# Reordering the two ends of a fused top-k attention and squared-ReLU kernel: one chunk of q turned ahead of k, and another order of the last step's work

## The chip, the cores and the metric

The kernel runs on one core of one Trainium2 chip. The metric is the device time of one execution in microseconds (us). Its engines are TensorE (PE, matrix multiply, with weight loads shown apart as PEld), VectorE (DVE), ScalarE (ACT), GpSimd (POOL) and SyncE (SP, which here only issues DMA). Each engine works through its own queue in order; semaphores tie the queues together.

## The reference

Top-k attention over 8 batches of 8 heads with 576 positions of 64 elements, followed by a feed-forward layer with a squared ReLU:

```python
B, H, S, D = q.shape                     # 8, 8, 576, 64
top_k = 32
scores = scale * np.matmul(q, k.transpose(0, 1, 3, 2))
kth = np.partition(scores, -top_k, axis=-1)[..., -top_k:-top_k + 1]
scores = np.where(scores >= kth, scores, -1000000000.0)
scores = scores - np.max(scores, axis=-1, keepdims=True)
attn = np.exp(scores)
attn = attn / (np.sum(attn, axis=-1, keepdims=True) + 1e-09)
x = np.matmul(attn, v)                   # then laid out as 4608 tokens x 512
h = np.maximum(x @ w_in, 0.0)            # w_in 512 x 2048
out = h * h @ w_out                      # w_out 2048 x 512
```

## The kernel before, in words

The work is cut into 144 steps (`U`). A step takes two tiles of 128 query rows (mostly the two heads of a pair, for one chunk `c` of the rows) against all 576 keys. For step u these things happen, each a function of its own:

- `prep_units(i)` turns the q and k of head pair i by PE transposes (L134 for the 128-row chunks, L146 for the last 64 rows) and copies them with a scale into `qkT` (L136 on DVE for the very first k, L138 and L149 on ACT for all others).
- `scores(u)` multiplies q with k in float32 into the two PSUM banks `sc_b` and `sc_a` (L202), and ACT copies them to SBUF as `s` (L207).
- `split(u)`, `join(u)` and `mins(u)` sort the 576 scores of a row into larger and smaller halves (DVE L238 to L250, POOL L257 to L269); `bring(u)` lets PE put a part of them back into PSUM (L223).
- `topk(u)` finds the 32 largest in four rounds of MAX8 (L288) and MATCH_REPLACE8 (L292) on DVE; the last round's MAX8 reads all 576 columns.
- `below(u, x)` marks what is under the threshold (ACT L334), `expo(u, x)` takes the exponentials of half x (ACT L343), `mask(u)` joins both (POOL L339), `turn(u)` transposes the weights by DMA into `wT`.
- `products(u)` multiplies them with v (PE L410: ten matmuls of 65 columns), `invert` takes the reciprocal of the sums (DVE L415, L421), `place` writes the scaled result into `x_tok` (ACT L438).

The feed-forward layer runs beside this in pieces: an "up" piece is 8 or 16 matmuls with `w_in` (PE L512) into one of two `gen` buffers, whose evacuation (`bend`: ACT L518, ReLU into `rl`) and square (POOL L526 or ACT L523) are put on the list `late` and written out by `flush()`. A "down" piece is four matmuls with `w_out` (PE L540) into the bank `dn_ps`; the last of four is followed by its own evacuation (ACT L547), also by way of `late`. Where there is no piece, `idle_piece()` lets PE multiply constants into `dn_ps` (L559).

There is no planner at run time. The program text is the order of every queue, and `pin` keeps it. There are three parts. Ahead of the loops, pair 0 is turned and the first two steps' scores are made. The first loop covers u below `Z` = 125, the second one u from 125 to 141. The last two steps, 142 and 143, are written out by hand. In step 143 the weights do not go through POOL and DMA: DVE masks them (`mask_last`, L377), PE transposes them (`turn_last`, L392), and ACT and DVE copy one half each (L395, L397). The last 128 tokens' feed-forward part is spread over the k-dimension as well: `x_last((kh,))` transposes one quarter of the tokens' 512 elements (PE L884, ACT L886), and `ups_last(bank, kh)` adds that quarter's eight matmuls (PE L891) into the two score banks, which are called `one` and `two` there. When all four quarters are in, `square_last` (ACT L896, DVE L898) and 32 final matmuls (PE L966) follow. `verify`, `note` (DVE L304, POOL L313 to L315) and the reductions at L947 to L950 gather flags that say whether the fast path's assumptions held.

The beginning ahead of the loops, in the order of the text:

```python
soon, coming = prep_units(0), 1
for _ in range(4):
    soon.pop(0)()
scores(0)
split(0)
join(0)
mins(0)
catch_up()
scores(1)
```

Of the kernel before, what the change touches and what calls it, by code (L numbers as in the profile page):

```python
# [22 lines left out]
def kernel(  # L23
# [22 lines left out]
    def pin(ins):  # L46
        tc.keep_in_program_order(ins)
        return ins
# [74 lines left out]
    def prep_units(i):  # L123
        q_raw, k_raw, v_raw = raw[i]
        qkT = heads.tile([128, 2, S], f32, name="qkT")
        va = vau[i % 6]
        prep[i] = (qkT, va)

        def main(which, src):
            def go():  # L130
                very_first = i == 0 and which == 1
                tp = ps_one.tile([128, 512], f32, name="gen", bufs=2)
                for c in range(4):
                    pin(nc.tensor.transpose(tp[:, c * 128:(c + 1) * 128], src[:, c], id_f[:, :]))  # L134
                if very_first:
                    pin(nc.vector.tensor_scalar(qkT[:, which, 0:512], tp[:, :], scalar1=EACH, scalar2=None, op0=ALU.mult))  # L136
                else:
                    pin(nc.scalar.activation(qkT[:, which, 0:512], tp[:, :], AF.Copy, scale=EACH))  # L138
                    owe(A=0.5)
            return go  # L140

        def rest(both=(0, 1), bank=None):
            tp = ps_one.tile([128, 512], f32, name="gen", bufs=2) if bank is None else bank
            for which in both:
                src = (q_raw, k_raw)[which]
                pin(nc.tensor.transpose(tp[:, which * 64:(which + 1) * 64], src[0:64, 4], id_f[0:64, 0:64]))  # L146
            owe(A=0.25)
            at = slice(both[0], both[-1] + 1)
            pin(nc.scalar.activation(qkT[:, at, 512:576], tp[:, 64 * both[0]:64 * both[-1] + 64].rearrange("p (w n) -> p w n", n=64), AF.Copy, scale=EACH))  # L149

        def values():
            owe(G=0.76)
            assert i < 6 or av_left[i - 6] == 0
            pin(nc.gpsimd.tensor_copy(va[:, :, :, 0:64], v_raw[:, :]))

        if i == 0:
            return [main(0, q_raw), main(1, k_raw), lambda: rest((1,), sc[0][:, 0, :]), values, lambda: rest((0,))]
        return [main(0, q_raw), main(1, k_raw), rest, values]


# [202 lines left out]
    def flush():  # L363
        while late:
            late.pop(0)()
# [281 lines left out]
    OLD = 2 * (U - GROUP)  # L647
    w_loads, w_casts = weight_units()
    scores(0)
    split(0)  # L650
    join(0)
    mins(0)
# [24 lines left out]
    for u in range(Z):  # L677
        now[0] = u
        f = u - 4
        lead = 2 if u > DEEP + 2 else 1  # L680
        pass_step()
        owe(A=4.5 if u < DEEP + 15 else 4.12, G=2.92)
        if u > 0:
            below(u - 1, 0)
        if u == 0:
            topk(0, (0, 1))
            split(1)
            join(1)
            topk(0, (2, 3))
        elif not DEEP < u < DEEP + 3:  # L690
            split(u + lead)
        if not DEEP < u < DEEP + 3:
            ahead(u + 1 + lead)
        if u > 0:
            topk(u, (0,))
        if u == DEEP + 2:
            join(u + 1)
            split(u + 2)
            ahead(u + 3)
            bring(u + 2)  # L700
        if ok(f) and f % 2:
            invert_two(f)
        if ok(f - 1):
            place(f - 1)
        if checks:
            note()
        if u == DEEP + 2:
            mins(u + 2)
        elif u != DEEP + 1:
            mins(u + lead)  # L710
        if u < DEEP + 3:
            catch_up()
# [36 lines left out]
        if u == DEEP:  # L749
            mins(u + 2)  # L750
            catch_up()
            ahead(u + 3)
            bring(u + 2)
        for _ in range(2 if u < 8 or u in (U - 22, U - 19) else 1):
            prepare(u)
        if 1 < u < 24 and not ups and not downs:
            idle_piece(2)
        turn_x(u)
        if w_casts and u >= 4:
            w_casts.pop(0)()  # L760
        if w_loads and u >= 1:
            w_loads.pop(0)()
# [9 lines left out]
    for u in range(Z, U - 2):  # L772
# [39 lines left out]
        expo(u, 0)  # L812
        if u == U - 4:
            piece()
            flush()
        expo(u, 1)
        flush()
        if u == Z:
# [52 lines left out]
        at = w[:, x, 0:S].bitcast(i32)  # L871
        pin(nc.gpsimd.tensor_tensor(at, at, marks[u % 2][:, x, :].bitcast(i32), op=ALU.add))
    turn(u)
    bend()
    square()
    empty(two)

    xl = ffp.tile([128, KH, 128], bf16, name="xT_1", bufs=2)
# [9 lines left out]
    def up_last(hp, f0, khs):  # L888
        for kh in khs:
            for n in range(4):  # L890
                pin(nc.tensor.matmul(out=hp[:, n * 128:(n + 1) * 128], lhsT=w_in[:, kh, (f0 + n) * 128:(f0 + n + 1) * 128],  # L891
                                     rhs=xl[:, kh, :], start=False, stop=(kh == 2 and n == 3)))

    def square_last(z, bank):
        rl = ffp.tile([128, 512], f32, name="rl", bufs=4)
# [20 lines left out]
    topk(u, (0, 1))  # L916
    expo_last(0)
    expo_last(1)
    bend()
    square()  # L920
    ups_last(one, 0)
    ups_last(two, 0)
    downs.pop(0)()
    topk(u, (2, 3))
    invert(u - 2)
    place(u - 2)
    mask_last(0)
    mask_last(1)
    turn_last(0)
    turn_last(1)  # L930
    x_last((1,))
    st[u]["o"] = ps_one.tile([128, 512], f32, name="gen", bufs=2)[:, 0:130].rearrange("p (x d) -> p x d", x=2)
    products(u)
    products(u - 1)
    invert(u)
    place_last(u)
    invert(u - 1)
    place_last(u - 1)
    x_last((3,))
    ups_last(one, 1)  # L940
    x_last((2,))
    ups_last(two, 1)
    ups_last(one, 3)
    ups_last(two, 3)
    verify(u)
    note()
    pin(nc.vector.tensor_reduce(worst[:, 0:1], flags[:, :, 0:OLD], axis=mybir.AxisListType.XY, op=ALU.max))  # L947
    sums_checked(nc.vector, OLD, 2 * U)
    pin(nc.vector.tensor_reduce(worst[:, 1:2], flags[:, :, OLD:2 * U], axis=mybir.AxisListType.XY, op=ALU.max))
    pin(nc.vector.tensor_scalar(worst[:, 0:1], worst[:, 0:1], scalar1=worst[:, 1:2], scalar2=0.0, op0=ALU.max, op1=ALU.is_gt))  # L950
    for z, bank in ((0, one), (2, two)):
        ups_last(bank, 2)
        for j in range(2):
            square_last(z + j, bank[:, j, :])
    downs.pop(0)()
# [144 lines left out]
```

## Time and profile before

| What | us |
|---|---|
| Median of 3 runs | 868.44 (867.41 to 871.32) |
| The profiled execution itself | 870.59 |
| Its span, from the first to the last instruction | 868.8 |
| DVE busy in the span | 837.7 (96%) |
| ACT busy | 810.6 (93%) |
| POOL busy | 797.5 (92%) |
| PE busy | 761.5 (88%) |

A line of a timeline gives start, duration, engine, source line, operation, written tile and read tiles with their shapes, the number of instructions merged, and in brackets the idle time in front of it with what ended it. A line of a table by stretches gives for each engine the busy time and, in brackets, the instructions; then the TensorE clock that was granted (1.00 is full), the share of the DMA engines and what they moved. Where a line of one source line's statistics appears, it gives the shortest, the median and the longest duration in ns, and the first and the last start. Matmul ends are modelled, so successive starts are the better measure of PE's pace.

### The profile page before, as it was taken

What the parts mean: (1) busy time and instruction counts of PE and PEld (TensorE: products, weight loads), DVE (VectorE), ACT (ScalarE), POOL (GpSimd) and SP (SyncE); (2) the same over time, 40 slices, a digit from 0 to 9 for tenths busy, and PEclk for the clock granted to TensorE, in tenths of its full rate; (3) what the DMA queues carried; (4) which work ended last, traced back from release to release, by engine and by line L of the source; (5) the groups of instructions that cost most, each with busy time, mean ns of one, the idle gap of its engine ahead of it and who ended that gap; (6) DMA issues with size and microseconds to landing.
All of it is one profiled execution on the core that took longest, in us unless ns stands there. A gap on an engine that the chain in (4) does not pass through costs nothing.

```text
span 868.8 us, 20017 instructions
## 1 busy us (share of the span) xinstructions
PE 761.5 (88%) x6038; PEld 484.6 (56%) x6038; DVE 837.7 (96%) x3427; ACT 810.6 (93%) x1635; POOL 797.5 (92%) x748
## 2 busy tenths in 40 slices
PE   6998997888888988889889888889898998999986
PEld 3554555555555545556555555556555654666654
DVE  5999999999999999999999999999999999999994
ACT  2887999999999999999999999999999999999982
POOL 3788999999999999999999999999999998999761
PEclk8999999999999999999999999999999999999998
DMA  5597776546556666356554565654565545423341
GB/s 122 125 228 156 185 172 109 121 101 114 95 106 114 120 120 121 67 112 121 109 120 96 113 115 98 124 116 105 114 128 109 117 100 107 87 58 86 73 84 44
DMA packets 325444, 98.06 MB, mean 113 GB/s; under 512 B 317520, under 2 KB 317776, under 8 KB 325328
## 3 DMA queue, kind: packets, MB, share of 16 engines
q1 hardware_dynamic: 323984, 96.28, 54.5%
q8 instruction: 49, 0.80, 0.4%
q14 instruction: 67, 0.55, 0.2%
q10 hardware_dynamic: 1344, 0.43, 0.2%
HBM read 36.70 MB, written 9.44 MB: 53 GB/s over the span
## 4 chain that ended last, share of the span: by engine, by line
DVE 56%; issue 12%; POOL 12%; PE 12%; ACT 7%; DMA 1%; SPq 0%; DVEq 0%; ACTq 0%; POOLq 0%
DVE m L288 25%; DVE cat L292 15%; DVE tops L238 7%; DVE cat L250 6%; POOL cat L257 5%; POOL cat L265 3%; ACT s L207 2%; PE sc_b L223 2%; PE sc_b L202 2%; PE gen L512 1%; POOL cat L269 1%; PE av_ps L410 1%; PE dn_ps L559 1%; ACT h L523 1%; PE dn_ps L540 1%
## 5 line engine op out<-in xcount | busy, mean ns | idle before, releaser
L288 DVE MAX8 m<-cat 128x8 f32<-128x100 f32 (+3 forms) x1152 | 435.1, 419 | 0.1
L292 DVE MATCH_REPLACE8 cat<-m,cat 128x100 f32<-128x100 f32 (+2 forms) x864 | 259.3, 308 | 0.3 <-issue 0.3
L265 POOL TENSOR_TENSOR cat<-s 128x576 int32<-128x576 int32 (+1 forms) x144 | 196.1, 1362 | 7.4 <-ACT s L207 7.1
L257 POOL TENSOR_TENSOR cat<-cat,tops 128x576 int32<-128x576 int32 (+1 forms) x144 | 196.0, 1361 | 1.9 <-DVE tops L238 0.8
L202 PE MATMUL sc_b<-qkT 64*128 64x288 f32 (+1 forms) x640 | 119.0, 449 | 33.7 <-DVE cat L250 24.3
L540 PE MATMUL dn_ps<-w_out,h 128*128 128x512 bf16 x560 | 143.3, 381 | 1.9 <-ACT wide L547 1.9
L223 PE MATMUL sc_b<-tops,id_f 128*128 128x144 f32 x528 | 96.6, 306 | 50.5 <-ACT s L207 50.2
L512 PE MATMUL gen<-xT,w_in 128*128 128x256 bf16 (+1 forms) x1088 | 128.5, 264 | 1.9 <-ACT rl L518 1.2
L512 PEld LDWEIGHTS <-w_in 128*128 128x128 bf16 x1344 | 109.9, 98 | 32.8 <-issue 19.9
L223 PEld LDWEIGHTS sc_b<-tops,id_f 128*128 128x128 f32 x528 | 73.4, 189 | 93.8 <-ACT s L207 90.3
L410 PEld LDWEIGHTS <-wT 128*128 128x128 bf16 (+3 forms) x1600 | 98.1, 99 | 47.0 <-issue 8.5
L334 ACT ACTIVATE marks_a<-s,m 128x576 bf16<-128x576 f32 x144 | 115.8, 812 | 0.0
L334 ACT ACTIVATE marks_b<-s,m 128x576 bf16<-128x576 f32 x142 | 110.4, 783 | 0.0
L202 PE MATMUL sc_a<-qkT 64*128 64x288 f32 (+1 forms) x640 | 109.1, 420 | 0.9 <-DVE tops L238 0.9
L207 ACT ACTIVATE s<-sc_b 128x576 f32<-128x576 f32 x144 | 94.8, 659 | 14.0 <-PE sc_b L202 8.6
L207 ACT ACTIVATE s<-sc_a 128x576 f32<-128x576 f32 x144 | 95.9, 666 | 6.6 <-PE sc_a L202 3.8
L238 DVE TENSOR_TENSOR tops<-sc_a,s 128x576 f32<-128x576 f32 x132 | 98.5, 746 | 0.0
L540 PEld LDWEIGHTS <-h 128*128 128x128 bf16 x560 | 47.7, 98 | 68.6 <-issue 31.3
L250 DVE TENSOR_TENSOR cat<-sc_b,tops 128x288 f32<-128x288 f32 x191 | 80.8, 443 | 5.2 <-PE sc_b L223 4.7
L518 ACT ACTIVATE rl<-gen 128x512 f32<-128x512 f32 x140 | 83.9, 599 | 1.0 <-PE gen L512 0.9
L202 PEld LDWEIGHTS sc_b<-qkT 64*128 64x128 f32 (+1 forms) x640 | 48.3, 176 | 61.6 <-DVE cat L250 33.2
L269 POOL TENSOR_TENSOR cat<-tops 128x288 int32<-128x288 int32 x97 | 77.8, 802 | 0.0
(133 smaller groups left out, 1358.4 us busy)
## 6 DMA issues: line engine op xcount, KB each, us to landing
out_dram<-wide SPq DMA_DIRECT2D x31, 256.0 KB, 2.7
q_raw<-in_q_dram SPq DMA_DIRECT2D x30, 256.0 KB, 3.7
k_raw<-in_k_dram SPq DMA_DIRECT2D x30, 256.0 KB, 3.7
h<-in_moe_w_in_dram SPq DMA_DIRECT2D x8, 512.0 KB, 5.3
h<-in_moe_w_out_dram SPq DMA_DIRECT2D x8, 512.0 KB, 4.2
v_raw_a<-in_v_dram SPq DMA_DIRECT2D x15, 256.0 KB, 4.1
v_raw_b<-in_v_dram SPq DMA_DIRECT2D x15, 256.0 KB, 4.0
out_dram<-wide SPq DMA_DIRECT2D x9, 128.0 KB, 2.5
```

The lines of the kernel that those rows point to most:

```text
L202: pin(nc.tensor.matmul(out=sc[j][r if rest else slice(0, 128), x, 0:HALF], lhsT=qkT[r, 0, c * 128:min(S, (c + 1) * 128)], rhs=qkT[r, 1, j ...
L207: pin(nc.scalar.activation(s[:, :, j * HALF:(j + 1) * HALF], sc[j][:, :, 0:HALF], AF.Copy))
L223: pin(nc.tensor.matmul(out=far[:, x, :], lhsT=id_f[:, :], rhs=st[w]["tops"][:, x, QUAR:HALF], start=True, stop=True))
L238: pin(tt(tops[:, :, :], one, two, op=ALU.max))
L250: pin(nc.vector.tensor_tensor(d["cat"][:, :, lo:lo + QUAR], far, d["tops"][:, :, 0:QUAR], op=op))
L257: pin(nc.gpsimd.tensor_tensor(at, at, top, op=ALU.subtract))
L265: pin(nc.gpsimd.tensor_tensor(at, s[:, :, 0:n], s[:, :, HALF:HALF + n], op=ALU.add))
L288: pin(nc.vector.max(out=m[r][:, x, :], in_=cat[:, x, at]))
L292: pin(nc.vector.match_replace(out=cat[:, x, at], in_to_replace=m[r][:, x, :], in_values=cat[:, x, at], imm_value=NEG))
L334: pin(nc.scalar.activation(marks[u % 2][:, x, :], d["s"][:, x, :], AF.Relu, bias=d["m"][3][:, x, 7:8], scale=-1.0))
L512: pin(nc.tensor.matmul(out=hp[:, n * n_rows:(n + 1) * n_rows], lhsT=w_in[:, kh, (f0 + n) * 128:(f0 + n + 1) * 128], rhs=xt(kh), start=(kh ...
L540: pin(nc.tensor.matmul(out=op[:, :], lhsT=held["h2"][:, f, c * 128:(c + 1) * 128], rhs=w_out[:, f, :], start=(f == 0), stop=(f == NF - 1)))
```

## The change

Four places change.

1. At the beginning only chunk 0 of q is transposed ahead of k, and copied by ACT as 128 columns. Chunks 1 to 3 are transposed behind the first scores (`soon.pop(0)()` behind `scores(0)`) and copied as 384 columns, between ACT's two score copies of step 0.
2. In step 0 an `idle_piece()`, four matmuls of 512 columns, goes in front of the scores of step 2.
3. In the second loop `flush()` is called between `expo(u, 0)` and `expo(u, 1)` in every step, where it was called in step 140 alone.
4. In the last two steps the order is changed: both pending `bend` and `square` calls come in step 142; the reciprocal of step 141 goes ahead of DVE's last round; `x_last((1,))` goes ahead of `turn_last(0)`, and `ups_last(one, 1)` between the two `turn_last`; `verify` and `note` go behind the masks; the products, reciprocals and placings of step 142 come ahead of those of 143; the quarters follow as 2, 3 with the matmuls of quarter 3 last.

```diff
-        def main(which, src):
+        def main(which, src, c0=0, c1=4):
...
-                for c in range(4):
+                at = slice(c0 * 128, c1 * 128)
+                for c in range(c0, c1):
...
-            return [main(0, q_raw), main(1, k_raw), lambda: rest((1,), sc[0][:, 0, :]), values, lambda: rest((0,))]
+            return [main(0, q_raw, 0, 1), main(1, k_raw), lambda: rest((1,), sc[0][:, 0, :]), values, main(0, q_raw, 1, 4), lambda: rest((0,))]
...
     scores(0)
+    soon.pop(0)()
     split(0)
...
             split(u + lead)
+        if u == 0:
+            idle_piece()
         if not DEEP < u < DEEP + 3:
             ahead(u + 1 + lead)
...
         expo(u, 0)
         if u == U - 4:
             piece()
-            flush()
+        flush()
         expo(u, 1)
...
     turn(u)
-    bend()
-    square()
+    for _ in range(2):
+        bend()
+        square()
     empty(two)
...
     expo_last(0)
     expo_last(1)
-    bend()
-    square()
     ups_last(one, 0)
     ups_last(two, 0)
     downs.pop(0)()
-    topk(u, (2, 3))
-    invert(u - 2)
+    topk(u, (2,), lambda: invert(u - 2))
+    topk(u, (3,))
     place(u - 2)
+    x_last((1,))
     mask_last(0)
     mask_last(1)
+    verify(u)
+    note()
     turn_last(0)
+    ups_last(one, 1)
     turn_last(1)
-    x_last((1,))
+    products(u - 1)
     st[u]["o"] = ...
     products(u)
-    products(u - 1)
+    invert(u - 1)
+    place_last(u - 1)
     invert(u)
     place_last(u)
-    invert(u - 1)
-    place_last(u - 1)
-    x_last((3,))
-    ups_last(one, 1)
     x_last((2,))
     ups_last(two, 1)
-    ups_last(one, 3)
-    ups_last(two, 3)
-    verify(u)
-    note()
+    x_last((3,))
+    ups_last(one, 2)
+    ups_last(two, 2)
...
     for z, bank in ((0, one), (2, two)):
-        ups_last(bank, 2)
+        ups_last(bank, 3)
```

More of the change, by code (lines that the diff above doesn't have):

```diff
@@ L132, in go @@
                 tp = ps_one.tile([128, 512], f32, name="gen", bufs=2)
-                for c in range(4):
+                at = slice(c0 * 128, c1 * 128)
+                for c in range(c0, c1):
                     pin(nc.tensor.transpose(tp[:, c * 128:(c + 1) * 128], src[:, c], id_f[:, :]))
                 if very_first:
-                    pin(nc.vector.tensor_scalar(qkT[:, which, 0:512], tp[:, :], scalar1=EACH, scalar2=None, op0=ALU.mult))
+                    pin(nc.vector.tensor_scalar(qkT[:, which, at], tp[:, at], scalar1=EACH, scalar2=None, op0=ALU.mult))
                 else:
-                    pin(nc.scalar.activation(qkT[:, which, 0:512], tp[:, :], AF.Copy, scale=EACH))
+                    pin(nc.scalar.activation(qkT[:, which, at], tp[:, at], AF.Copy, scale=EACH))
                     owe(A=0.5)
@@ L891, in up_last @@
                 pin(nc.tensor.matmul(out=hp[:, n * 128:(n + 1) * 128], lhsT=w_in[:, kh, (f0 + n) * 128:(f0 + n + 1) * 128],
-                                     rhs=xl[:, kh, :], start=False, stop=(kh == 2 and n == 3)))
+                                     rhs=xl[:, kh, :], start=False, stop=(kh == KH - 1 and n == 3)))
     def square_last(z, bank):
```

## The prediction

> **What bounds the kernel now.** I read the page first, then the busy time by stretches, then the chain that ended last, then the timelines of the first 35 us and the last 25 us, where the diff works. The profiled execution took 870.59 us, its span 868.8 us, so 1.8 us lie around it; it stands 2.15 us above the median of the three runs, 868.44 us.
>
> ```profile
> core 0: us, PE busy (x) PEld busy (x) DVE busy (x) ACT busy (x) POOL busy (x), PEclk, DMA share, GB/s
> 100.00:735.00 635.00, 555.30 (x4410) 355.44 (x4410) 631.93 (x2599) 626.48 (x1268) 625.35 (x574) 1.00 0.57 114
> 735.00:810.00 75.00, 71.54 (x619) 48.55 (x620) 70.04 (x293) 71.90 (x151) 72.75 (x67) 0.98 0.35 73
> 850.00:869.00 19.00, 11.27 (x114) 9.18 (x114) 6.60 (x16) 4.02 (x11) 0.78 (x3) 0.86 0.10 32
> ```
>
> From 100 to 735 us DVE is busy 631.93 of 635 us, with ACT and POOL close behind; to 810 us POOL, ACT and PE are each over 95%. These long stretches are a belt: what reaches them earlier leaves them earlier, and nothing in the diff shortens them. Only ahead of the belt and behind it (850 to 869 us, DVE busy 6.60 of 19) is there time that order alone can change. The built order agrees: POOL and SP keep their order to the last instruction, DVE differs in a few places behind step 142, PE and ACT at the head, ACT in nine steps of the second loop, PE in the tail.
>
> **Head: k 0.33 us earlier.** In the chain, q's landing releases eight transposes (L134), then DVE's copy of k, then the first scores.
>
> ```profile
> L134 PE MATMUL gen<-id_f,q_raw x4: 351/418/444, 6.0 to 6.7; 128*128 128x128 f32 x4
> L134 PE MATMUL gen<-id_f,k_raw x4: 272/273/273, 6.9 to 7.2; 128*128 128x128 f32 x4
> 7.54 0.69 DVE L136 TENSOR_SCALAR qkT<-gen 128x512 f32<-128x512 f32 x1 [7.54 <-PE gen L134]
> 8.37 0.76 PE L202 MATMUL sc_b<-qkT 64*128 64x288 f32 x4 [0.67 <-DVE qkT L136]
> 8.93 0.68 PE L202 MATMUL sc_a<-qkT 64*128 64x288 f32 x4
> 11.91 0.76 PE L202 MATMUL sc_b<-qkT 64*128 64x288 f32 x4 [2.29 <-ACT s L207]
> ```
>
> The four of q start 0.22 us apart (6.04 to 6.71), the four of k 0.11 (6.90 to 7.23): PE speeds up near 6.9 us. With three q transposes gone, k's start at 6.28, 6.5, 6.7 and 6.9, the last 0.33 us before 7.23; DVE's copy, the scores and everything behind follow. (If the speed-up came first, 3 x 0.11 = 0.33 too; if after, 3 x 0.22 = 0.66.) The three transposes moved behind the first scores, and their copy on ACT, lie between the end of the scores at 9.61 and the second scores at 11.91, 2.29 us in which PE only waits: 0.33 us on PE, and on ACT less than the 0.69 that DVE takes for 512 columns, say 0.6, ahead of a copy that waits for DVE's third split operation anyway. Cost: nothing; without that cover 0.33 + 0.6, some 0.9 us. No DMA moves.
>
> **Head: the idle piece.** Four 128x512 matmuls go in behind the second scores, ahead of the q tail and the third scores.
>
> ```profile
> 13.00:14.00 1.00, 0.17 (x3) 0.00 (x0) 1.00 (x5) 0.35 (x1) 0.53 (x1) 0.84 0.00 0
> 14.00:15.00 1.00, 0.00 (x0) 0.00 (x0) 1.00 (x4) 0.34 (x1) 0.00 (x0) 0.50 0.14 33
> 15.45 1.33 PE L202 MATMUL sc_b<-qkT 64*128 64x288 f32 x4 [2.28 <-ACT qkT L149]
> 16.54 1.20 PE L202 MATMUL sc_a<-qkT 64*128 64x288 f32 x4
> 17.67 3.40 PE L559 MATMUL dn_ps<-fill,id_h 128*128 128x512 bf16 x8
> 18.46 0.47 DVE L240 TENSOR_TENSOR sc_b<-sc_a,s 128x288 f32<-128x288 f32 x1 [0.39 <-ACT s L207]
> 30.59 0.82 DVE L250 TENSOR_TENSOR cat<-sc_b,tops 128x288 f32<-128x288 f32 x2 [0.62 <-PE sc_b L223]
> ```
>
> PE stands 2.28 us, and the granted clock falls to 0.50 at 13.7 us (a mean of 0.84 over its microsecond). Under it the third scores start 1.09 us apart instead of the 0.56 of the first ones (8.37 to 8.93), DVE waits 0.39 us for their copy, and the eight fillers take 3.40 us (0.43 each), which sends the next pair's copies, and with them ACT's whole queue, late; the 0.62 us before 30.59 is that lateness arriving at DVE. The new matmuls take 4 x 0.43 = 1.7 us at worst, within the 2.28. If they hold the clock, both waits go: 0.39 + 0.62 = 1.01 us. Bounds 0 and 1.01; I take 1.01: from 11.91 to 15.45 PE works some 1.3 of 3.5 us now, and with the fillers 2.2 (at full clock) to 3.0. The Trainium skill, "TensorE: Matmul & The Clock Gate", section "What's actually happening", lets the clock fall only after a window of some 3.4 us of idling; by it these 2.28 us cost nothing, the fillers bring nothing and the sum below would be 2.8 us. The trace disagrees: 0.50 within 2.28 us of waiting.
>
> **Second loop: bend between the two exps.** `flush()` now runs in every step between `expo(u, 0)` and `expo(u, 1)`; nine times an L518 or L547 evacuation moves ahead of the second exp, four times an L523 square with it. ACT's sum per step is the same; no wait is added if the PE piece is done by then.
>
> ```profile
> 776.35 1.04 PE L540 MATMUL dn_ps<-w_out,h 128*128 128x512 bf16 x4
> 777.88 0.76 PE L223 MATMUL sc_b<-tops,id_f 128*128 128x144 f32 x4 [0.50 <-ACT s L207]
> 778.72 0.89 ACT L343 ACTIVATE w_two_a<-s,low 128x576 bf16<-128x576 f32 x1
> 780.23 0.17 DVE L415 RECIPROCAL shares<-av_ps 128x2 f32<-128x2 f32 x1 [0.94 <-PE av_ps L410]
> DVE cat L250 <- PE sc_b L223: 2.4, 4, 0.9
> DVE shares L415 <- PE av_ps L410: 2.2, 3, 1.0
> ```
>
> In this step the piece ends at 777.39, the first exp at 779.6: 2.2 us of room. DVE's waits here (2.4 and 2.2 us in all from 735 to 812 us) end on PE, which waits for ACT's score copies, and these come as late as before, since the same work precedes them. Where a square has moved, x_tok comes later by it, at most the exp's 0.9 us; the PE transposes that read x_tok in two steps have 0.50 us of idle behind them, so 0.4 us each can be lost. I take 0, between a gain of 2.3 us (half of those waits) and a loss of 0.8.
>
> **Tail.** Times in the frame of the trace before.
>
> ```profile
> 846.64 0.62 PE L891 MATMUL sc_a<-xT,w_in 128*128 128x128 bf16 x8
> 847.09 0.61 PE L891 MATMUL sc_b<-xT,w_in 128*128 128x128 bf16 x8
> 848.59 1.31 POOL L526 TENSOR_TENSOR h<-rl 128x512 bf16<-128x512 f32 x1 [1.29 <-ACT rl L518]
> L377 DVE SCALAR_TENSOR_TENSOR w_two_c<-s,m,marks_b x2: 797/1196/1594, 848.2 to 848.9; 128x576 bf16<-128x576 f32 x2
> 849.06 0.45 PE L392 MATMUL gen<-id_h,w_two_c 128*128 128x128 bf16 x5 [0.49 <-DVE w_two_c L377]
> 850.57 0.45 PE L392 MATMUL gen<-id_h,w_two_c 128*128 128x128 bf16 x5 [1.06 <-DVE w_two_c L377]
> 851.06 0.49 DVE L397 COPY wT<-gen 128x640 bf16<-128x640 bf16 x1 [0.55 <-PE gen L392]
> 851.44 0.78 PE L410 MATMUL gen<-vau_b,wT 128*128 128x65 bf16 x10 [0.36 <-ACT xT L886]
> 852.15 0.79 PE L410 MATMUL av_ps<-vau_a,wT 128*128 128x65 bf16 x10
> 853.68 1.06 PE L891 MATMUL sc_b<-xT,w_in 128*128 128x128 bf16 x8
> 854.53 1.06 PE L891 MATMUL sc_a<-xT,w_in 128*128 128x128 bf16 x8
> 857.21 1.08 ACT L896 ACTIVATE rl<-sc_a 128x512 f32<-128x512 f32 x2 [3.01 <-PE sc_a L891]
> 857.40 1.03 PE L540 MATMUL dn_ps<-w_out,h 128*128 128x512 bf16 x4
> 858.59 0.61 PE L966 MATMUL av_ps<-w_out,h 128*128 128x256 bf16 x4
> 849.00:852.00 3.00, 1.52 (x20) 1.10 (x20) 2.00 (x2) 0.98 (x2) 0.90 (x1) 1.00 0.06 13
> 853.00:854.00 1.00, 1.00 (x14) 0.78 (x13) 0.71 (x3) 0.35 (x2) 0.13 (x1) 0.68 0.00 0
> 856.00:857.00 1.00, 1.00 (x14) 1.00 (x12) 0.31 (x2) 0.00 (x0) 0.00 (x0) 0.61 0.00 0
> ```
>
> First the mask. Its two passes take 0.80 and 1.59 us; the second runs under POOL's square, itself 1.31 us long, and ends 0.62 us after it. The moved `bend` puts that square at about 847.3 to 848.3, before the passes: the second then ends at 848.97 + 0.8 = 849.8 instead of 850.5. "SBUF — State Buffer", section "SBUF: two separate sides", of the Trainium skill, says that a DVE instruction with two SBUF inputs and a GpSimd one exclude each other; the rows fit (849.90 + 0.6 = 850.5).
>
> Then PE's order. Transposes of half 0 to 849.5; the eight matmuls of `ups_last(one, 1)` fill the wait for half 1, at 0.5 to 0.6 us, to 850.1 (x_tok for its transpose stands at 848.9, as before); half 1 to 850.55 and its copy, beside it, to 851.1; ten products of step 142 and ten of 143, 0.71 apart, to 852.05. Until here 0.17 us are won against 852.22, but the second ten products, which end at 852.94 now, are in it, and one group of eight. Behind it: transpose 0.22, `two 1` 0.45, transpose 0.23 (its place, 0.53 behind the products as before, is ready at 852.6), `one 2`, `two 2` 0.45 each, `one 3` 0.5: ended at 854.4, where now the last `one` group releases ACT's L896 at 857.2. The 0.45 is that of 846.64 to 847.09, at full clock; at 0.50, as from 853.4 to 856.8 now, a group costs 0.85 (853.68 to 854.53). From there the rest is unchanged: `two 3` 0.45, then from the down piece's start to the final matmuls 1.19 (857.40 to 858.59), so these start at 854.4 + 1.64 = 856.05 instead of 858.59: **2.5 us**. The checks that DVE and POOL bring forward (`least` 0.33, note) fall into DVE's 0.55 us wait before L397; if they didn't fit, 0.3 us.
>
> If the clock falls all the same, three groups and `two 3` cost 0.4 more each, 1.6: 0.9 us is left. I take 2.5, since PE, busy 1.52 of the 3 us from 849 to 852 now, has no gap over 0.4 us there in the new order.
>
> Sum: 0.33 + 1.01 + 0 + 2.5 = 3.84 us; the profiled execution would be 866.75 us, the median 868.44 - 3.84 = **864.6 us**, 0.44% less. A measurement of this kernel can tell about 0.5%, 4.3 us, from no change.
>
> **Rivals.** (1) The clock falls in the tail: gain 0.33 + 1.01 + 0.9 = 2.2, 866.2 us. For it: the products' short 65-column matmuls keep PE half used, and they are there still. Against: the gaps are filled. 0.20. (2) The fillers don't hold the clock at the head: 3.84 - 1.01 = 2.8, 865.6 us. The 2.3 us of waiting from 9.6 to 11.9 stay. 0.12. (3) Freed `gen` buffers let PE run ahead in the second loop and half of DVE's waits on PE go: 2.3 more, 862.3 us. For it the rows at 780.23; against it, PE and ACT are full there. 0.10. (4) Slower: the early bend finds its piece unfinished, ACT waits at it with the second exp, the masks and the score copies queued behind, in a stretch where ACT and POOL are full. A whole piece, 1.04 us, in nine steps is 9.4 us: 874.0 us. It decides once the piece ends after the first exp; the 2.2 us of room speak against. 0.08.
>
> The forecast itself has 0.50, by itself 863.1 to 866.1 us (the unit costs, and runs that lie up to 2.9 us from their median). The range, 862.0 to 868.6, takes in rivals 1 to 3 and the lower bounds (0.33 alone is 868.1) and leaves out rival 4 and the far ends. Faster by over 0.5%, below 864.1: four tenths of the forecast's 0.50, most of rival 3, a little of the rest: 0.30. Slower by over 0.5%: 0.08. Within: 0.62.
>
> **What would show it.** DVE's first L240 at 9.5 us instead of 9.85; granted clock 1.00 from 13 to 20 us, no wait at the third L240 nor before the L250 near 30; the second L377 pass at 0.8 us; `one 3` ending some 4.6 us behind the second pass (now 6.6), at clock 1.00; from 100 to 735 us the same DVE sum. I am wrong if DVE's waits between 735 and 812 us change by over 1 us, if ACT waits at L518 there, or if the final matmuls start less than 1.5 us nearer to the last MAX8.

## The result and the profile after

The changed kernel took 865.36 us (median of 5 runs, 864.96 to 865.88), the kernel before 869.83 us beside it (5 runs, 867.41 to 871.32): a ratio of 0.9948, 95% interval 0.9926 to 0.9970. In a second comparison (run e10 below) it was 865.13 against 868.33 us, 0.9955 (0.9938 to 0.9973). The forecast was 864.6 us in 862.0 to 868.6, or 0.44% less; whether the gain is above or below 0.5% these runs do not settle. The kernel before scatters more: its medians in four comparisons lie between 868.33 and 870.86 us, its single runs between 866.8 and 874.25 us; the changed kernel's 15 runs lie between 863.59 and 866.16.

The profiled execution after took 865.07 us with a span of 863.3 us, 5.5 us less than the one before. Line numbers are one higher than before up to the middle of the file (L202 is now L203, L240 L241, L250 L251, L410 L411), and 5 or less higher in the tail (L891 is L896, L377 L378, L966 L969).

The head, from the timeline after:

```profile
6.97 0.69 DVE L137 TENSOR_SCALAR qkT<-gen 128x512 f32<-128x512 f32 x1 [6.97 <-PE gen L135]
7.81 0.76 PE L203 MATMUL sc_b<-qkT 64*128 64x288 f32 x4 [0.67 <-DVE qkT L137]
9.28 0.47 DVE L241 TENSOR_TENSOR sc_b<-sc_a,s 128x288 f32<-128x288 f32 x1 [1.62 <-ACT s L208]
9.56 0.49 ACT L139 ACTIVATE qkT<-gen 128x384 f32<-128x384 f32 x1 [0.31 <-PE gen L135]
12.52 1.04 PE L560 MATMUL dn_ps<-fill,id_h 128*128 128x512 bf16 x4
14.88 0.76 PE L203 MATMUL sc_b<-qkT 64*128 64x288 f32 x4 [1.12 <-ACT qkT L150]
15.44 0.68 PE L203 MATMUL sc_a<-qkT 64*128 64x288 f32 x4
16.05 2.12 PE L560 MATMUL dn_ps<-fill,id_h 128*128 128x512 bf16 x7
17.42 0.44 DVE L241 TENSOR_TENSOR sc_b<-sc_a,s 128x288 f32<-128x288 f32 x1
```

DVE's first L241 comes 0.57 us earlier than before (9.85); the four new matmuls take 1.04 us; the third scores start 0.56 us apart (before 1.09); the third L241 comes 1.04 us earlier (before 18.46) and waits for nothing.

The busy time by stretches after, with columns as in the prediction; the clock is the first number behind the five engines:

```profile
core 0: us, PE busy (x) PEld busy (x) DVE busy (x) ACT busy (x) POOL busy (x), PEclk, DMA share, GB/s
13.00:14.00 1.00, 0.76 (x4) 0.19 (x2) 1.00 (x4) 0.00 (x0) 0.00 (x0) 1.00 0.00 0
14.00:15.00 1.00, 0.12 (x2) 0.15 (x4) 1.00 (x5) 0.77 (x2) 0.17 (x1) 1.00 0.00 0
40.00:100.00 60.00, 55.31 (x373) 31.85 (x379) 58.42 (x238) 50.15 (x96) 49.07 (x40) 0.97 0.83 189
71.20:74.50 3.30, 3.30 (x14) 1.84 (x13) 2.10 (x14) 2.10 (x3) 3.22 (x4) 0.50 0.53 106
100.00:735.00 635.00, 549.67 (x4351) 355.91 (x4407) 631.58 (x2596) 626.22 (x1267) 625.39 (x573) 1.00 0.58 113
149.70:153.00 3.30, 3.14 (x14) 1.66 (x16) 3.30 (x20) 1.15 (x2) 3.30 (x4) 0.50 0.00 0
735.00:810.00 75.00, 71.47 (x632) 49.28 (x641) 71.70 (x299) 73.43 (x155) 74.50 (x69) 1.00 0.37 73
```

The head's clock is held, but two falls stand where the trace before has none: at 71 us DVE is busy 2.10 of 3.30 us, and at 150 us. From 735 to 810 us DVE does 1.7 us more work than before (71.70 against 70.04) in the same time. The waits of DVE from 735 to 812 us after (total, times, longest):

```profile
DVE shares L416 <- PE av_ps L411: 2.4, 4, 1.0
DVE cat L251 <- PE sc_b L224: 0.6, 2, 0.3
```

That is 3.0 us where it was 4.6 (2.2 and 2.4). The tail, from the timeline after:

```profile
844.24 2.05 POOL L527 TENSOR_TENSOR h<-rl 128x512 bf16<-128x512 f32 x2
844.32 1.33 SPq L383 DMA_TRANSPOSE wT<-w_two_b  x1
844.63 0.62 PE L896 MATMUL sc_a<-xT,w_in 128*128 128x128 bf16 x8
846.24 1.53 DVE L378 SCALAR_TENSOR_TENSOR w_two_c<-s,m,marks_b 128x576 bf16<-128x576 f32 x2
847.39 0.61 PE L896 MATMUL sc_a<-xT,w_in 128*128 128x128 bf16 x8
847.84 0.45 PE L393 MATMUL gen<-id_h,w_two_c 128*128 128x128 bf16 x5
848.98 0.79 PE L411 MATMUL av_ps<-vau_a,wT 128*128 128x65 bf16 x10 [0.70 <-DMA wT<-w_two_b]
849.70 0.79 PE L411 MATMUL gen<-vau_b,wT 128*128 128x65 bf16 x10
850.50 0.61 PE L896 MATMUL sc_b<-xT,w_in 128*128 128x128 bf16 x8
852.04 0.61 PE L896 MATMUL sc_a<-xT,w_in 128*128 128x128 bf16 x8
852.75 1.09 ACT L901 ACTIVATE rl<-sc_a 128x512 f32<-128x512 f32 x2 [1.12 <-PE sc_a L896]
854.13 0.61 PE L969 MATMUL av_ps<-w_out,h 128*128 128x256 bf16 x4
```

Both squares now run ahead of the masks, whose two passes take 1.53 us together (before 0.80 and 1.59). The groups of `ups_last` start 0.45 us apart, at full clock. New is PE's wait of 0.70 us for the DMA transposition of step 142, which lands 4.6 us behind its issue at 844.32. From the first group (844.63) to the first final matmul (854.13) it is 9.50 us; before, 11.95 (846.64 to 858.59).

Where a profile stands ahead or behind is read best from the start of a step's first MAX8. In the first line are times of the trace before, below them differences to it (minus is earlier); then the tail from its first group to its first final matmul, the stretch from the last matmul's start to the span's end, and the falls of the clock to 0.50, by the trace's clock record (us from the span's start). One more fall, which every profile has behind the last matmul, is left out. e1 to e12 are the runs of the next section:

```
                 step 4  step 10 step 11 step 124 step 132 step 140 | tail  | end  | clock at 0.50
before            37.88   73.21   79.24   725.86   774.32   827.21  | 11.95 | 6.8  | 13.7-20.5, 737.3-740.7, 853.4-856.8
after             -1.78   -1.78   -0.69    -0.21    -1.34    -2.01  |  9.50 | 5.8  | 71.1-74.5, 149.6-153.1
e10 (after again) -1.75   -1.75   -0.76    -0.21    -1.33    -1.89  |  9.44 | 5.7  | 71.2-74.6, 149.7-153.2, 736.8-740.2
e1 split only     -0.91   -0.92   -0.35     0.10    -1.01    -1.00  | 11.67 | 6.8  | 11.7-18.5, 73.1-76.5, 138.0-141.4, 151.6-155.0, 325.7-329.1, 851.4-854.8
e2 idle only      -0.09   -0.09    1.13     1.39     0.71     0.41  | 10.44 | 5.4  | 11.2-18.1, 72.7-76.1
e3 loop only       0.94    0.95    0.93     1.25     0.17    -0.41  | 12.98 | 6.1  | 11.5-21.7, 151.4-154.9, 738.5-742.0, 851.2-858.0
e4 tail only       0.61    0.60    0.60     0.64     0.59     0.59  | 11.36 | 6.2  | 10.8-21.1, 737.9-741.3, 853.9-857.3
e5 tail fill       0.78    0.78    0.77     1.27     0.20     0.22  |  9.85 | 5.7  | 11.2-21.4, 151.1-154.5, 840.6-844.0
e6 square early   -0.28   -0.28    0.29     0.81    -0.29    -0.29  | 11.30 | 6.9  | 12.5-19.3, 73.9-77.4, 138.8-142.2, 152.5-155.9, 326.5-329.9, 852.2-855.6
e7 two early      -1.49   -1.49   -1.51    -1.17    -1.82    -2.78  |  9.47 | 5.9  | 12.5-15.9, 149.1-152.5, 736.2-739.6
e8 more fill      -2.02   -2.01   -2.02    -2.01    -3.22    -3.88  |  8.63 | 5.8  | 323.3-326.8
e9 both           -1.78   -1.78   -1.80    -1.25    -2.43    -3.10  |  9.07 | 5.8  | 136.0-142.8
e11 own first     -1.84   -1.83   -1.84    -1.58    -2.75    -3.40  |  9.14 | 5.5  | none
e12 no idle        1.21    1.21    1.19     1.68     1.05     0.10  |  9.97 | 6.7  | 8.2-21.9, 151.6-155.0
```

So the 5.5 us between the two profiles are: 1.78 won at the head, 1.57 of it given back by step 124; 1.80 won from step 124 to 140; 2.45 in the tail; 1.05 behind the last matmul, a stretch that took 5.4 to 6.9 us in the profiles with the old order of the tail and 5.5 to 6.7 in those with the new one.

### The profile page after: what moved, and what is told of

Read it like the earlier page. It is cut to its first block, busy times and chain, and to the rows that moved or that the text cites. A ratio compares the mean times of both kernels' runs of the same rounds, so it can differ in the third digit from the quotient of the medians.

```text
span 863.3 us, 19942 instructions
## 1 busy us (share of the span) xinstructions
PE 751.6 (87%) x5960; PEld 483.2 (56%) x6042; DVE 836.7 (97%) x3427; ACT 810.5 (94%) x1636; POOL 797.9 (92%) x748
## 4 chain that ended last, share of the span: by engine, by line
DVE 48%; POOL 19%; issue 13%; PE 12%; ACT 4%; DMA 2%; SPq 0%; POOLq 0%; DVEq 0%; ACTq 0%
DVE m L289 21%; DVE cat L293 13%; POOL cat L258 8%; DVE tops L239 6%; DVE cat L251 5%; POOL cat L266 5%; POOL cat L270 2%; PE gen L513 2%; PE sc_b L224 2%; PE sc_b L203 2%; PE dn_ps L541 2%; PE av_ps L411 2%; POOL w_two_b L340 1%; ACT s L208 1%; PE sc_a L203 1%
## 5 line engine op out<-in xcount | busy, mean ns | idle before, releaser
L203 PE MATMUL sc_b<-qkT 64*128 64x288 f32 (+1 forms) x640 | 118.6, 450 | 32.9 <-DVE cat L251 25.2
L541 PE MATMUL dn_ps<-w_out,h 128*128 128x512 bf16 x492 | 131.6, 380 | 7.0 <-issue 3.5
L513 PEld LDWEIGHTS <-w_in 128*128 128x128 bf16 x1344 | 109.9, 98 | 32.2 <-issue 19.3
L411 PEld LDWEIGHTS <-wT 128*128 128x128 bf16 (+3 forms) x1600 | 97.8, 99 | 49.9 <-issue 8.0
L203 PE MATMUL sc_a<-qkT 64*128 64x288 f32 (+1 forms) x640 | 109.1, 422 | 0.7 <-DVE tops L239 0.7
L251 DVE TENSOR_TENSOR cat<-sc_b,tops 128x288 f32<-128x288 f32 x191 | 80.8, 443 | 4.2 <-PE sc_b L224 3.7
L203 PEld LDWEIGHTS sc_b<-qkT 64*128 64x128 f32 (+1 forms) x640 | 48.1, 176 | 58.9 <-DVE cat L251 30.9
```

What stands on the lines that cost most here:

```text
L203: pin(nc.tensor.matmul(out=sc[j][r if rest else slice(0, 128), x, 0:HALF], lhsT=qkT[r, 0, c * 128:min(S, (c + 1) * 128)], rhs=qkT[r, 1, j ...
L251: pin(nc.vector.tensor_tensor(d["cat"][:, :, lo:lo + QUAR], far, d["tops"][:, :, 0:QUAR], op=op))
L513: pin(nc.tensor.matmul(out=hp[:, n * n_rows:(n + 1) * n_rows], lhsT=w_in[:, kh, (f0 + n) * 128:(f0 + n + 1) * 128], rhs=xt(kh), start=(kh ...
L541: pin(nc.tensor.matmul(out=op[:, :], lhsT=held["h2"][:, f, c * 128:(c + 1) * 128], rhs=w_out[:, f, :], start=(f == 0), stop=(f == NF - 1)))
```

## The experiments

**Each part alone (e1 to e4).** First the late q chunks: `main` and the list of pair 0 as in the change, and `soon.pop(0)()` behind `scores(0)`.

> The kernel before with only the first part of the change: chunk 0 of q turned ahead of k, chunks 1 to 3 behind the first scores. Theory (each end of the kernel pays for itself): DVE's first L241 starts 0.3 to 0.6 us earlier than 9.85 us, the third scores, which carry the 2.28 us of PE idleness, are still there with the granted clock at 0.50, and the time falls by 0.3 to 0.6 us. Rival A (the belt from 40 to 735 us, where DVE has over a microsecond of waits, swallows what the head wins): first L241 earlier all the same, the time unchanged. Rival B (the clock's fall comes by a grid of its own, whatever the order): the fall near 13.7 us may be missing here too, and the time falls by 1 us or more.

Measured: 870.77 us against 870.86, ratio 1.0002 (0.9985 to 1.0020). DVE's first L241 stood at 9.14 us, but the third scores still started 1.09 us apart at half clock, and at 73.1 us another fall took 0.57 us. In this profile what the head wins does not reach the end (rival A in effect): 0.91 us ahead at step 4, 0.10 behind at step 124, with falls of the clock between. Over all runs the interval, from 1.3 us less to 1.7 us more, leaves the theory's 0.3 to 0.6 us open.

The idle piece alone:

```diff
             split(u + lead)
+        if u == 0:
+            idle_piece()
```

> The kernel before with only the second part of the change: four 128x512 matmuls in front of the scores of step 2. Theory: first L240 at 9.85 as before, granted clock 1.00 from 13 to 20 us, no DVE wait at the third L240 nor before the L250 near 30 us, 1.0 us less. Rival A: the belt swallows it, same time. Rival B (the four matmuls do not hold the clock; the third scores start 1.09 us apart as before): 0 to +0.5 us.

Measured: 868.37 us, ratio 0.9983 (0.9968 to 0.9999). So there is a gain, but the profile does not have it where the theory does (it is 0.09 us ahead at step 4):

```profile
11.30:18.00 6.70, 6.17 (x21) 3.16 (x21) 5.82 (x25) 2.28 (x5) 3.17 (x4) 0.50 0.13 30
7.82:11.23 3.41, 1.24 (x8) 0.78 (x8) 1.79 (x6) 0.89 (x3) 0.77 (x2) 1.00 0.66 148
848.00:858.00 10.00, 7.95 (x98) 5.63 (x97) 7.32 (x17) 4.75 (x12) 2.09 (x4) 1.00 0.35 33
```

The clock fell at 11.2 us, ahead of the new matmuls; the 3.41 us before had PE busy for 1.24 only. So this execution does not show whether they hold the clock where it falls later, as at 13.7 us in the trace before. The third row is of use below: here the tail of the kernel before runs at full clock, and takes 10.44 us instead of 11.95.

The early `flush` alone:

```diff
         if u == U - 4:
             piece()
-            flush()
+        flush()
         expo(u, 1)
```

> The kernel before with only the third part: the evacuation of a finished piece between the two exps of every step of the second loop. Theory: 0, between -0.8 and +0.8 us; DVE's waits from 735 to 812 us change by less than 1 us. Rival (freed buffers let PE run ahead): 1.6 to 2.3 us less, and DVE's waits on PE there halve, 4.6 to 2.3 us. Other rival (ACT waits at the evacuation): slower by 1 us or more, with ACT idle in front of L518 between 735 and 812 us.

Measured: 870.34 us, ratio 0.9999 (0.9983 to 1.0014). The trace shows more. From step 124 to 140 the lead grows by 1.66 us, and DVE's waits for L223 are, first in the kernel before from 725 to 776 and from 800 to 828 us, then here from 800 to 828 us (from 727 to 776 us there is none of it left):

```profile
DVE cat L250 <- PE sc_b L223: 1.2, 2, 0.7
DVE cat L250 <- PE sc_b L223: 0.9, 1, 0.9
```

```profile
DVE cat L250 <- PE sc_b L223: 0.3, 1, 0.3
```

Of this, 0.66 us come in one place, at step 137, and there all eight profiles with the early `flush` gain 0.66 or 0.67 us, and the five without it (e1, e2, e4 to e6) nothing. Near 800 us the kernel before has:

```profile
800.31 0.60 ACT L547 ACTIVATE wide<-dn_ps 128x512 f32<-128x512 f32 x1
800.96 1.02 PE L540 MATMUL dn_ps<-w_out,h 128*128 128x512 bf16 x4 [0.64 <-ACT wide L547]
```

The evacuation of `dn_ps` stands behind the second exp, PE waits 0.64 us for it, and the scores behind that piece come late to DVE (the 0.9 above). In e3 the evacuation stands ahead of the second exp, at 799.89, PE starts the piece at 800.55 without waiting, and DVE's wait is 0.3. The 0.64 is in all six profiles without the early `flush` and in none with it. So a freed buffer does let PE run ahead, as the rival has it, but it is worth a third of the rival's price. The other 1.08 us, from step 124 to 132, are no gain of the `flush` alone: e1, e2, e5 and e6 have 0.7 to 1.1 there without it, since only the trace before and e4 lose that much under a fall of the clock at 737 us. With the early `flush` such a fall costs little (e3 and e10, 1.08 and 1.12 gained) or about half (e7, 0.65). In the trace before PE waits 0.59 us there for a `gen` buffer (L518), in e3 and e10 it does not. ACT waits in front of no L518. The medians cannot show 0.66 us, with an interval of 1.3 us to either side.

The tail alone (`bend` and `square` twice in step 142, and the order of step 143 as in the change):

> The kernel before with only the fourth part: the order of the last two steps. Theory: 2.5 us less, the final matmuls 2.5 us nearer to the last MAX8 (before 11.79 us behind its start, then 9.3), granted clock 1.00 up to them, and the ten products of step 142 waiting 0.5 to 0.9 us for the DMA transposition. Rival (most of the gain is that no clock fall happens to lie in the tail in the runs seen): where the clock falls there, 0.9 us less only; where it stays, 2.5.

Measured: 869.12 us, ratio 0.9985 (0.9966 to 1.0004). In its profile the clock falls at 853.9, the rival's case:

```profile
852.06 0.79 PE L410 MATMUL av_ps<-vau_a,wT 128*128 128x65 bf16 x10 [1.18 <-DMA wT<-w_two_b]
855.10 1.06 PE L892 MATMUL sc_b<-xT,w_in 128*128 128x128 bf16 x8
```

The tail takes 11.36 us, 0.6 less than before instead of 2.45; 0.48 of the loss is the longer wait for the DMA, most of the rest groups of 0.85 us. Theory and rival (2.5 and 0.9 us) both lie inside the interval of the runs, 3.0 us less to 0.3 more. By their ratios the four parts add up to 0.31% where the whole is 0.45 to 0.52%; with some 0.15% to either side on each, this does not tell whether they simply add.

**Clock or order in the tail (e5, e6).** Matmuls of zeros in the waits of PE, the order untouched (`hold_clock(bank, n)` adds n of 512 columns to a bank):

```diff
+    hold_clock(two, 2)
     turn_last(0)
+    hold_clock(one, 4)
     turn_last(1)
     x_last((1,))
+    hold_clock(two, 1)
```

> The kernel before with its own order of the tail, and seven matmuls of zeros put into the waits of PE there (two in front of the first turned half, four between the halves, one in front of the products); they add nothing to the banks. Theory (what the change won in the tail is some 1.0 us by order and some 1.5 us by the clock that does not fall): the granted clock stays 1.00 from 849 us to the final matmuls, from the first L893-type group to the first final matmul 10.45 us instead of 11.95, and over all runs some 1 us less than before, since the fall in the tail is not in every run. Rival (order wins all of the 2.5 us): the stretch stays between 11.5 and 12 us and the time is the same.

Measured: 868.64 us against 870.12, ratio 0.9980 (0.9967 to 0.9994). The tail ran at full clock and took 9.85 us:

```profile
849.00:858.00 9.00, 8.65 (x99) 6.08 (x100) 5.36 (x14) 4.35 (x12) 2.04 (x4) 1.00 0.15 28
```

The clock is as the theory has it, but this is one execution, and in e2 the same order ran at full clock without zeros: that they hold it is not shown. The tail is another 0.59 us below 10.44. Here the square began when the second mask pass was half through, and this pass took 0.81 us; that a fall at 840.6 us had shifted the queues against each other is the likely reason.

The second square alone moved ahead:

```diff
     turn(u)
-    bend()
-    square()
+    for _ in range(2):
+        bend()
+        square()
...
     expo_last(1)
-    bend()
-    square()
```

> The kernel before with only the second pending bend and square moved ahead of the masks, as the change has it. Theory (DVE and POOL get in each other's way over the mask): the second mask pass takes 0.8 us instead of 1.59, the second turned half starts 0.7 to 0.8 us earlier, the time falls by 0.7 us where the clock is the same. Rival (the products of step 142 and the quarters behind them wait for the DMA transposition anyway, landing some 4.6 us behind its issue): the mask is shorter, the final matmuls come less than 0.3 us earlier.

Measured: 868.46 us, ratio 0.9974 (0.9959 to 0.9988).

```profile
847.91 1.52 DVE L377 SCALAR_TENSOR_TENSOR w_two_c<-s,m,marks_b 128x576 bf16<-128x576 f32 x2
849.49 0.45 PE L392 MATMUL gen<-id_h,w_two_c 128*128 128x128 bf16 x5 [0.28 <-DVE w_two_c L377]
```

Both passes take 1.52 us, PE waits 0.28 us for the second half instead of 1.06, and the tail takes 11.30 us, 0.65 less, with a fall of the clock in it as before. The theory's 0.7 is met in this stretch, and the DMA does not hide it in that order. Over all runs the gain is 1.0 to 3.6 us; what is beyond 0.7 this edit does not explain.

**The new wait, and the falls further ahead (e7, e8).** `ups_last(two, 1)` ahead of `products(u - 1)` instead of behind `x_last((2,))`:

> The changed kernel with the second group of quarter 1 ahead of the products instead of behind them, so that it lies in PE's 0.70 us wait for the DMA transposition. Theory: the wait in front of the products falls to 0.25 us, the final matmuls come 0.45 us earlier (9.05 us behind the first group of quarter 0, where the changed kernel has 9.50), the time is 0.45 us under that of the changed kernel (ratio to before about 0.9943). Rival (something behind the products, the placing on DVE or the turned quarter, ends last): no earlier.

Measured: 864.58 us against 870.12, ratio 0.9937 (0.9912 to 0.9961), but a tail of 9.47 us, 0.03 less:

```profile
848.18 0.79 PE L411 MATMUL av_ps<-vau_a,wT 128*128 128x65 bf16 x10 [0.23 <-DMA wT<-w_two_b]
850.28 0.23 PE L889 MATMUL gen<-id_h,x_tok 128*128 128x128 bf16 x1 [0.42 <-DVE x_tok L909]
```

The wait for the DMA shrinks as the theory says, and the group is missed where it stood: PE now waits 0.42 us for DVE's placing. In this profile the rival is right. The constant matmuls of e8:

```diff
     soon.pop(0)()
+    idle_piece()
     split(0)
...
+        if u == 23:
+            idle_piece(4, "gen", 2)
...
         if u == DEEP:
             mins(u + 2)
             catch_up()
+            idle_piece(5)
...
+        if u == Z:
+            idle_piece(3, "gen", 2)
         bring(u + 2)
```

> The changed kernel with constant matmuls in four more waits of PE: four behind the first scores and the late q chunks, five in step 9 (the 1.60 us in front of the scores at 70.9 us), four in step 23 (the 1.93 us in front of those at 149.9 us), three in step 125. Theory (the clock falls at the ends of a grid of 3.41 us that runs freely, after a stretch in which PE streamed little, and each fall early in the kernel gives back up to 1.1 us of what the head won): no fall at 71 or 149 us in the profile, mean clock 0.997 or above, DVE's sum from 40 to 100 us as short as before less 1.1 us more, and 0.5 to 1.2 us under the changed kernel (ratio to before about 0.994 to 0.9935). Rival (these falls lie where DVE is ahead, so they cost nothing; or the new matmuls delay the scores): same time as the changed kernel or up to 1 us more.

Measured: 863.44 us, ratio 0.9923 (0.9899 to 0.9946). The granted clock, by stretches:

```profile
6.00:323.00 317.00, 278.57 (x2077) 171.41 (x2105) 313.67 (x1280) 294.12 (x580) 291.42 (x263) 1.00 0.64 133
327.00:859.00 532.00, 468.37 (x3880) 309.02 (x3931) 518.83 (x2128) 512.22 (x1050) 498.85 (x459) 1.00 0.52 103
```

No fall at 71 or 150 us, and the lead of 2.02 us at step 4 is there at step 124 (2.01). The one fall left, at 323 us, cost nothing (2.03 ahead of it, 2.04 behind). That is the theory, and it shows what the changed kernel gave back. Its tail of 8.63 us has another cause: here the DMA transposition lands 3.7 us behind its issue, and the products wait for nothing.

**Against the changed kernel on one chip (e9 to e12).** Medians: before 868.33 us.

> The constant matmuls of the run e8 and the early second group of the run e7 together. Theory (fills take away the falls of the clock ahead of the last steps, the early group shortens the tail by 0 to 0.45 us, depending on when the DMA transposition lands): 0 to 0.45 us under the run e8, ratio to before 0.9918 to 0.9923. Rival (e8's lead came from a lucky landing of its DMA transposition, 3.7 us behind the issue where the changed kernel has 4.6): 0.5 to 0.9 us above e8, ratio 0.993.

Measured: 863.71 us, 0.9946 (0.9928 to 0.9965), 1.4 us under the changed kernel of the next run (e10). Its tail is 9.07 us, 0.44 longer than e8's, with the DMA landing at 3.9 us: the products wait for nothing, and PE again waits 0.42 us for DVE's placing. So the theory is wrong on the group. On the fills it is right but for one place: a fall from 136.0 to 142.8 us takes 0.52 us.

> The changed kernel once more, for comparison with the others of this call on one chip. Theory: as at first, 0.9948 of before, and in its second profile falls of the clock at other places than 71 and 149 us or the same, each at the end of a stretch of 3.41 us, with DVE's lead over the kernel before cut by some 1.1 us at a fall near 71 us. Rival (the places of the falls belong to the kernel): falls at 71 and 149 us to the same tenth of a microsecond.

Measured: 865.13 us, 0.9955 (0.9938 to 0.9973). The profile repeats the falls at 71 and 149 us within 0.1 us and loses 0.99 us at the first; since its first full clock also comes within 0.1 us of the other's (6.38 and 6.28 us), this pair alone decides nothing between theory and rival. The other profiles do: counted from the first full clock, the falls at 71 to 77 us come 64.85 us (after, e10) or 68.27 us (e1, e2, e6) later, 19 and 20 times 3.413. So the falls follow that moment, and not the place in the kernel alone.

> The run e9 with the products of step 143 ahead of those of step 142 again, as in the kernel before, and the quarters in the order 3, 2. Theory (the products of step 142 wait for a DMA transposition that lands 3.6 to 5.1 us behind its issue, those of 143 only for DVE's copy): no wait for the DMA in the tail, and 0.1 to 0.5 us under e9. Rival (DVE's copy of the second half ends as late as the DMA lands): the same to 0.2 us.

Measured: 863.32 us, 0.9945 (0.9923 to 0.9966), 1.8 us under e10 and 0.4 under e9, which their scatter does not tell apart. As the theory has it, no product waits for the DMA; the tail is the same to 0.07 us all the same, as the rival has it. It is the only profile without a fall ahead of the last matmul:

```profile
5.60:858.90 853.30, 748.71 (x5967) 481.67 (x6048) 836.55 (x3427) 809.40 (x1635) 794.74 (x727) 1.00 0.57 114
```

> The changed kernel without the idle piece in front of the scores of step 2. Theory (it is what holds the clock at the head, together with the late q chunks): the clock falls between 10 and 18 us, the third scores start 1.1 us apart instead of 0.56, DVE reaches step 4 by 0.7 to 1.1 us later than in the changed kernel, and the time is 1.0 to 1.5 us above it. Rival (the late q chunks alone hold it): the same time as the changed kernel.

Measured: 867.33 us, 0.9978 (0.9962 to 0.9995), 2.2 us over e10. The clock is at 0.50 from 8.2 to 21.9 us, the third scores start 1.09 us apart, and step 4 comes 2.96 us later than in e10: the theory, at twice its price. But this fall begins ahead of the place of the idle piece (12.5 us in the trace after), so the piece could have shortened it at most, and the profile overstates the price. The 2.2 us over all runs are the better measure.

The versions with fills (e9, e11) beat both kernels. e8 and e7 were not compared with the changed kernel directly, so between e8, e9 and e11 nothing is settled. The order of e8's tail is the shortest where the DMA transposition lands early (8.63 us at 3.7); where it lands at 5.1 (e12), the same order takes 9.97.

## Why the prediction came out

**k earlier, 0.33.** Right in mechanism and size. At full clock throughout, the first transpose of k starts 0.46 us behind the first of q in the old order (e2) and 0.14 behind it in the new (e1): 0.32. The 0.57 of the profile holds more than that, since the clock rose earlier (6.28 us, before 6.86); with the old head DVE's first L240 stands anywhere from 9.58 to 9.86 us in six profiles.

**Idle piece, 1.01.** Right where the forecast looked: no wait at the third L241, clock 1.00 from 13 to 20 us, no wait before the L251 near 30 us; the lead is 1.78 at step 4, against 1.34 forecast for both. But this clock is in part chance: in e6, whose head is that of the kernel before, it is back at 19.3 us instead of 20.5, and the wait near 30 us is gone without the four new matmuls. Rival 2 came in a form that was not written: the clock fell at the head with the fillers alone (e2), with the late q chunks alone (e1), and once with both (e7). The step behind it failed: "what reaches them earlier leaves them earlier" does not hold from 40 to 100 us, where DVE is idle 1.58 of 60 us and a fall of the clock at 71 us takes 1.09 us. Another 0.48 us goes by step 124, 0.20 of it at the fall near 150 us. Then 0.21 us are left.

**Second loop, 0.** This step failed: DVE's waits were to stay because the score copies "come as late as before, since the same work precedes them". PE did not wait for score copies alone, but also for evacuations behind the second exp (0.64 us near 801 us in the trace before), and those now come earlier. DVE's waits fell from 4.6 to 3.0 us, beyond the 1 us named as the mark of an error. The profile gains 1.80 us, inside the bounds (2.3 to -0.8): 0.66 by the early `flush`, and 1.13 mostly because the trace before has a fall at 737 us and this one has not. Rival 4 has no trace: no wait of ACT at L518.

**Tail, 2.5.** The sum is right (2.45), and so are its parts: at equal clock the old order takes 10.44 us (e2), the new one 9.50, so order won 0.94 (forecast 0.9), and 1.51 (forecast 1.6) is a fall of the clock that was in one profile and not in the other. What failed is the reason for the second part, that the new order keeps the clock up by filling the gaps: the old order ran at full clock in e2, the new one fell in e4. That these two profiles differed so was luck. Rival 1 is thus another execution of the same order, and e4 was 1.86 us longer than the changed kernel (0.48 of them the DMA's) where 1.6 was written. The sum also let the products of step 142 run first at the landing that the trace before happens to show (3.6 us behind the issue). At 4.6 us they wait 0.70, at 5.1 (e4) 1.18; without a wait the new order takes 8.63 (e8). The mask's 0.7 was right (e6: 0.65), though the exclusion fits the rows only roughly: a pass of 0.80 begun behind the square's end at 849.90 would have ended at 850.7, and it ended at 850.5. `one 3` ended 4.9 us behind the second pass, forecast 4.6.

So the total was near by luck: a head that was too high by what was given back (1.13) met a second loop that was too low (1.80). What the two profiles differ by beyond that, 1.05 us behind the last matmul, is the scatter of that stretch.

## What to carry to other kernels

Before an earlier start is booked at the end, follow it through each stretch in which the bounding engine still waits; a table of one instruction's start, step by step, shows where a lead is lost. Look up what ends each wait, not one of them in place of all. A profile's fall of the clock is a property of that execution: put a tail or a head at full and at half clock into the sum as two cases, and compare orders only between profiles with the same clock. Where the order of two consumers is swapped, the landing of each one's transfer is a term of the sum.

## What the runs showed of the hardware

**The clock falls by a grid, after stretches in which PE was busy about half the time or less.** All falls listed in the table last 3.41 us or a multiple, and within a profile they lie multiples of 3.413 us apart. The stretches of 3.41 us ahead of three falls (before at 13.7 us, after at 71.1 and 149.6 us) had PE busy about half the time or less, a fourth (before at 853.4 us) more than two thirds, with ten-fold 65-column matmuls in it:

```profile
10.28:13.69 3.41, 1.26 (x9) 0.92 (x9) 3.41 (x18) 1.30 (x2) 1.58 (x2) 1.00 0.39 89
849.95:853.36 3.41, 2.43 (x35) 1.94 (x35) 1.80 (x6) 0.80 (x3) 0.00 (x0) 1.00 0.00 0
```

```profile
67.72:71.13 3.41, 1.76 (x16) 1.08 (x17) 3.41 (x10) 1.95 (x4) 3.33 (x3) 1.00 1.26 237
146.23:149.64 3.41, 1.71 (x20) 1.35 (x18) 3.41 (x11) 3.41 (x8) 3.41 (x5) 1.00 0.51 99
```

The Trainium skill, "TensorE: Matmul & The Clock Gate", section "What's actually happening", gives a window of 3413 ns that runs freely and does not start anew with a kernel; by that the traces agree, and so the same kernel can have other falls in another execution. It names an idle window as the cause; the rows above had none. Cut into stretches of 3.413 us from the first full clock on, the fourteen traces have 3440 stretches at full clock. All 21 with PE busy under 0.515 of the time were followed by a fall, 15 of the 103 from 0.515 to 0.605, and three of the 3316 above, all three with the 65-column matmuls of the last two steps in them. So the limit lies near half for most of this kernel's work; what exactly is counted these runs do not tell.

The mean granted clock goes with the kernels (before 0.988 to 0.990 over the runs of a comparison, changed 0.994, e11 0.998). Within the kernel before it goes with the scatter in one comparison (23 runs: correlation -0.82, 3.2 us between those up to 0.989 and those above), hardly in the two others (-0.28 and 0.08). What else moves its time stays open.

**The same DMA transposition lands 3.6 to 5.1 us behind its issue.** In the changed kernel's trace a packet of instructions (16 KB, 0.96 us from 846.33) falls into it, the rate drops below 12 GB/s ahead of a last burst, and it lands at 4.6 us; in the kernel before the packet comes at 849.29, when the last data packet is through, and it lands at 3.6. Such a packet comes near this transposition in all fourteen profiles, and the landing goes with its place, told in us behind the issue:

| The packet comes | Profiles | Landing |
|---|---|---|
| at 0.58, 0.68 and 0.68, begun ahead of the data | e8, e9, e11 | 3.7, 3.9, 3.9 |
| at 1.29 to 2.01, among the data | after, e10, e7, e2 | 4.6 |
| at 2.97 and 2.98, when the last data packet is through | before, e5 | 3.6 |
| at 3.05 to 3.08, with three to five data packets still to end | e1, e3, e4, e6, e12 | 5.1 |

In the last row these data packets end within 0.02 us behind the packet of instructions. Both profiles of the changed kernel have it at the same place (2.01 and 1.96), so the landing may belong to the program. That the packet causes the delay is a reading of these traces; no run moved it alone.
